# Moving the gates, the weight loads and some decoding around the first experts of a fused attention, MoE and MLP kernel

## The chip, the cores and the metric

The kernel runs on one core of a Trainium2 chip. The metric is the device time of one execution in microseconds (us), as the median of several runs. TensorE has two clock levels, 1.2 and 2.4 GHz; the profile shows the granted clock as a share of the higher one.

## The reference

```python
kv   = einsum('bhsd,bhse->bhde', k, v)            # 4 batches, 8 heads, 576 rows, head size 64
out  = einsum('bhsd,bhde->bhse', q, kv)
attn = out / sqrt(mean(out*out, -1) + 1e-6) * g_norm
x    = attn as [2304, 512]

logits = normed(x) @ normed(expert_emb).T / tau   # 8 experts
e      = argmax(logits, 1); gate = softmax(logits)[e]
x[i]   = gate[i] * (relu(x[i] @ w1[e]) @ w2[e])   # w1 512x1024, w2 1024x512, for the one expert of a row

h = x @ w_in                                       # 512 x 2048
g = max(h, 0) + log1p(exp(-abs(h)))
y = g @ w_out                                      # 2048 x 512, float32 result
```

## The kernel before

**Head.** Attention runs over 18 tiles of 128 rows (`tiles`); its steps are ordered by a small list planner (`step`, `list_schedule`), which takes for each step its engine, an estimated duration, what it depends on and a `tail`, a length of work that is known to follow it. Each finished tile `xa` is stored to `xd` in DRAM. `st_xo` multiplies a tile by g_norm and `st_n` (ScalarE) sums its squares into `ssx`, which only the gates need. Six of these tiles come last, behind the routing. The routing (`top1`, `slots`, `tokens`, `count`, `ranks`, `indices`) sorts the experts by their counts, so that rank 0 is the largest; `CAPS` are the row capacities by rank, 368 down to 280. `rk_idx` holds the row numbers of each rank and `rk_e` the expert of each rank. `offsets` works out where each rank's rows stand in the sorted order `x2`; `gates` works out the gate of each row from `ssx` and the logits.

**Experts.** For each rank r: `gather` fetches the rows from `xd` by an indirect DMA of GpSimd, in three parts of up to 128 rows; `transposes` brings them to the column layout and splits them into a high part `xh` (ScalarE) and a low part `xl` (VectorE). For rank 0 this is `first_transposes`, in pieces. A product of two split operands takes three matmuls (`three`). Eight column blocks m of w1 give `hh` (ScalarE, relu) and `hl` (VectorE); then, in eight steps f, w2 is applied into four output tiles `accs`. Column blocks and output tiles share a ring of five PSUM tiles, so the four tiles of `accs` are those that held column blocks 3 to 6. The weights of an expert come as eight tiles of 512 KB, four of w1 and four of w2 (`load_w`, on SyncE's queue; the expert is read from `rk_e`). `split_w` makes `wh` by a cast on ScalarE and `wl` by a subtraction on GpSimd or VectorE. Before the change, rank 0 has tiles 0 and 2 on GpSimd and the six others on VectorE; the other ranks have all on GpSimd.

Work that is not of the expert itself is called from hooks: `hook1(r, m)` after each column block and `hook2(r, f)` after each f step. They split the weights of rank r+1, load those of rank r+2 (some calls later, through `later` and `now`), gather rank r+2, transpose rank r+1, and run pieces of `pre_decode`. That decodes the 64-bit MLP weights in 32 halves of seven steps, one on ScalarE and six on VectorE, for which it uses a temporary tile in PSUM.

**Gates before.** `gates` is called in three lots around `first_transposes`, ahead of the first expert; `gate_table` sorts the gates by rank in three steps. Rank 0's outputs are multiplied by `gate_row` on VectorE; every other rank has its gathered rows scaled on ScalarE (`scale`), rank 1 at m = 5 to 7 of rank 0, and its outputs copied into `x2` by ScalarE. `row_ids` and `store_ids` write the row numbers to DRAM for the final scatter.

**MLP.** Five blocks of 512 columns of `x2` (`split_x`) go through `mlp_step`, two of which run inside the last expert. The outputs are scattered by an indirect DMA with `idx2`, which is made from the stored row numbers and from `own` and `keep` (the case that a capacity is exceeded).

The queues are those of the engines: each takes its instructions in the order written. The order around the change, ahead of the first expert:

```python
    for c in range(3):
        gather(0, c)
    for i in range(2):
        load_w(0, i)
    nc.sync.dma_start(out=seen, in_=xgs[0][0:1, 2, 0:1])   # holds SyncE until the third part has landed
    for i in range(2, 8):
        load_w(0, i)
```

Of the kernel before, what the change touches and what calls it, by code (L numbers as in the profile page):

```python
# [17 lines left out]
ALU = mybir.AluOpType  # L18
# [7 lines left out]
def attention_moe_mlp(tc, q, k, v, g_norm, emb, tau, w1, w2, w_in, w_out, out, caps=CAPS):  # L26
# [108 lines left out]
    gate_row, ga_row, rf_row = (early[:, 76 * NT + 384 * i:76 * NT + 384 * i + 384] for i in range(3))  # L135
# [50 lines left out]
    with ExitStack() as hs:  # L186
# [223 lines left out]

        def st_xo(t, eng):
            if eng == "G":
                nc.gpsimd.tensor_tensor(out=xo_t[t % NXO], in0=xa_t[t], in1=g_rep.rearrange("p h d -> p (h d)"), op=ALU.mult)
            else:
                nc.vector.tensor_tensor(
                    out=xo_t[t % NXO].rearrange("p (h d) -> p h d", d=D),
# [123 lines left out]
        def indices():  # L540

            pt = tp.tile([128, E, 3, E], F32, name="pt")
            nc.vector.tensor_tensor(
                out=pt,
                in0=tab.rearrange("p e c -> p c e").unsqueeze(1).to_broadcast([128, E, 3, E]),
                in1=perm.unsqueeze(2).to_broadcast([128, E, 3, E]),
                op=ALU.mult,
            )
            yield
            with nc.allow_low_precision("small integers"):  # L550
                nc.vector.tensor_reduce(out=rk_idx, in_=pt, axis=AX.X, op=ALU.add)
            yield
# [51 lines left out]
        def route(g):  # L604
# [18 lines left out]
            if last_:  # L623
# [6 lines left out]
                step(("idx", 0), "D", 269, lambda g_=gen_: next(g_), ("tab", g), ("rank", 4))  # L630
                step(("idx", 1), "D", 269, lambda g_=gen_: next(g_), ("idx", 0), tail=5000)
# [29 lines left out]
        for u in range(NXD, NT):  # L661
            step(("xo", u), "D", 700, lambda u=u: st_xo(u, "D"), ("idx", 1), ("xa", u), ("nn", u - NXO))
            step(("nn", u), "A", 613, lambda u=u: st_n(u), ("xo", u))
# [99 lines left out]
        drain(offsets())  # L763
    head.close()

# [333 lines left out]

    def first_transposes():  # L1100
# [5 lines left out]
        def transposes_of(c):  # L1106
            n = min(128, C - 128 * c)
            for kk in range(KD):
                nc.tensor.transpose(parts[-1][kk][:, 128 * c:128 * c + n], xgs[0][:n, c, kk * 128:kk * 128 + 128], ident[:n, :n])
# [37 lines left out]
    def gate_rows():  # L1147

        ga = ga_row.rearrange("p (c n) -> p c n", n=128)
        nc.vector.tensor_copy(ga, rk_gate[:, 0, :].unsqueeze(2).to_broadcast([128, 3, 128]))  # L1150
        yield
        p = tp_tile()
        for c in range(3):
            n = min(128, caps[0] - 128 * c)
            nc.tensor.transpose(p[:, c * 128:c * 128 + n], ga[:n, c, :], ident[:n, :n])
        nc.scalar.copy(gate_row[:, :caps[0]], p[:, :caps[0]])
        yield

    gr = gate_rows()
# [20 lines left out]

    def hook1(r, m):
        now()
        if r == 0:
            if m in (2, 3):
                next(gq)
            if m in (4, 7):
                next(gr)
            if m in (1, 5):
                next(ri)
            if SC <= m < SC + 3:  # L1190
                scale(1, m - SC)
# [7 lines left out]
        if m % 2 == 1:  # L1199
            first_half(r, m // 2 - (r == 0))  # L1200

    def hook2(r, f):
        now()
        if r + f == 0:
            first_half(r, 3)
# [7 lines left out]
        if 2 <= f < 6:  # L1213
# [3 lines left out]
        if f == 4:  # L1217
            store_ids(r)
        if r == E - 1:
            if f < KD:  # L1220
                split_x(0, f)
# [8 lines left out]
    def expert(r):  # L1230
# [4 lines left out]
        for m in range(NM1):  # L1235
# [8 lines left out]
            if r in (1, 7):  # L1244
# [10 lines left out]
        if r:  # L1255
            off = nc.scalar.value_load(rk_off[0:1, r:r + 1], min_val=0, max_val=XCOL - C)
        if r == E - 1:
# [173 lines left out]
```

## Time and profile before

| | |
|---|---|
| time, median of 3 runs | 740.52 us (740.25 to 741.89) |
| the profiled execution's own time | 742.71 us |
| its span, first to last instruction | 740.9 us |
| mean granted clock of TensorE | 0.982 |
| busy: TensorE, VectorE, ScalarE, GpSimd | 705.3, 514.8, 407.7, 265.1 us |

The rows below come from the profiled execution; times in them count from the start of its span. PE is TensorE, PEld its weight loads, DVE VectorE, ACT ScalarE, POOL GpSimd, and SPq the DMA queue of SyncE. An instruction's row gives its start, its duration, its engine, its line in the kernel, its operation, the tiles that it writes and reads, and their shapes. A bracket says how long the engine was idle before it and what ended that. L872 is the subtraction that makes `wl`, L870 the cast that makes `wh`.

### The profile page before, as it was taken

The numbers are of one execution on the slowest core, as the hardware profiler recorded it, in microseconds if no ns is written. First come the engines' busy times: TensorE is split into PE (matmuls) and PEld (weight loads), VectorE is DVE, ScalarE is ACT, GpSimd is POOL, SyncE is SP. The second block draws the span as 40 slices with busy tenths as digits, with TensorE's granted clock in tenths as the row PEclk, the third lists the DMA queues.
The fourth block names the chain that finished last, engine by engine and source line by source line (L and its number), as shares of the span: only waits on it lengthen the run. The fifth ranks groups of instructions, "written<-read, shape, count | busy, mean of one in ns | idle before, by whom it ended". The sixth has DMA issues, their size and how long they took to land. (4 is left out here: it accounts for less than half of the span.)

```text
span 740.9 us, 11430 instructions
## 1 busy us (share of the span) xinstructions
PE 705.3 (95%) x4180; PEld 619.2 (84%) x4180; DVE 514.8 (69%) x944; ACT 407.7 (55%) x753; POOL 265.1 (36%) x201
## 2 busy tenths in 40 slices
PE   7987489999999999998999999999999999999995
PEld 4977289989999999997888888888888888888894
DVE  3579894988688788897787665656656656566563
ACT  2768466547656567565564654436444454445553
POOL 6234457766786877673463020000200020000201
PEclk9999789999999999999999999999999999999999
DMA  8994599898797988830220010000100000000100
GB/s 240 274 264 168 180 311 315 245 324 267 266 301 258 330 275 290 304 106 32 82 86 31 0 58 1 0 1 1 57 1 0 1 36 22 1 1 0 58 1 32
DMA packets 66912, 96.66 MB, mean 130 GB/s; under 512 B 12948, under 2 KB 41644, under 8 KB 66850
## 3 DMA queue, kind: packets, MB, share of 16 engines
q1 hardware_dynamic: 63330, 86.02, 37.3%
q0 software_dynamic: 3344, 9.80, 3.6%
q8 instruction: 35, 0.57, 0.3%
q14 instruction: 27, 0.22, 0.1%
q10 hardware_dynamic: 176, 0.05, 0.0%
HBM read 78.01 MB, written 17.84 MB: 129 GB/s over the span
## 5 line engine op out<-in xcount | busy, mean ns | idle before, releaser
L872 POOL TENSOR_TENSOR wl<-st,wh 128x1024 fp32r<-128x1024 f32 x66 | 159.6, 2420 | 73.4 <-ACT wh L870 72.8
L977 POOL DMA_INDIRECT out_dram<-orow,idx x18 | 18.5, 1028 | 317.2 <-ACT orow L976 314.1
L940 DVE TENSOR_SCALAR u<-e 128x512 f32<-128x512 f32 (+1 forms) x78 | 31.1, 399 | 123.6 <-ACT e L939 123.5
L938 ACT ACTIVATE e<-tp_t 128x512 f32<-128x512 f32 (+1 forms) x76 | 42.5, 559 | 127.9 <-PE tp_t L866 127.8
L870 ACT CAST wh<-st 128x1024 fp32r<-128x1024 f32 x72 | 75.3, 1047 | 45.5 <-POOL wl L872 21.0
L864 PE MATMUL acc_t<-hh,wh 128*128 128x368 f32 (+7 forms) x256 | 81.2, 317 | 1.7 <-DVE hl L1246 1.6
L864 PE MATMUL acc_t<-xh,wh 128*128 128x368 f32 (+7 forms) x256 | 79.4, 310 | 2.6 <-DVE xl L1117 2.3
L865 PE MATMUL acc_t<-xl,wh 128*128 128x368 f32 (+7 forms) x256 | 78.9, 308 | 0.0
L866 PE MATMUL acc_t<-xh,wl 128*128 128x368 f32 (+7 forms) x256 | 78.8, 308 | 0.0
L865 PE MATMUL acc_t<-hl,wh 128*128 128x368 f32 (+7 forms) x256 | 78.0, 305 | 0.0
L866 PE MATMUL acc_t<-hh,wl 128*128 128x368 f32 (+7 forms) x256 | 78.0, 305 | 0.0
L946 ACT ACTIVATE u<-u 128x512 f32<-128x512 f32 (+1 forms) x78 | 46.1, 591 | 44.0 <-DVE e L942 43.3
L959 DVE TENSOR_TENSOR gl<-u,gh 128x512 fp32r<-128x512 f32 (+1 forms) x78 | 58.0, 743 | 3.0 <-ACT gh L958 3.0
L865 PE MATMUL tp_t<-xs,wh 128*128 128x512 f32 (+1 forms) x160 | 59.0, 369 | 0.6 <-DVE xs L882 0.6
L866 PE MATMUL tp_t<-xs,wl 128*128 128x512 f32 (+1 forms) x160 | 58.9, 368 | 0.0
L864 PE MATMUL tp_t<-xs,wh 128*128 128x512 f32 (+1 forms) x160 | 58.8, 368 | 0.0
L990 PE MATMUL acc_t<-wh,gl 128*128 128x512 f32 x144 | 56.2, 391 | 1.3 <-DVE gl L959 1.3
L988 PE MATMUL acc_t<-wh_b,gh 128*128 128x512 f32 x144 | 56.2, 390 | 0.6 <-ACT gh L958 0.6
L866 PE MATMUL tp_t<-xs,wl_b 128*128 128x512 f32 (+1 forms) x152 | 56.6, 372 | 0.0
L865 PE MATMUL tp_t<-xs,wh_b 128*128 128x512 f32 (+1 forms) x152 | 56.6, 372 | 0.0
L864 PE MATMUL tp_t<-xs,wh_b 128*128 128x512 f32 (+1 forms) x152 | 56.6, 372 | 0.0
L988 PE MATMUL acc_t<-wh,gh 128*128 128x512 f32 x144 | 56.1, 390 | 0.0
(260 smaller groups left out, 1808.4 us busy)
## 6 DMA issues: line engine op xcount, KB each, us to landing
st<-in_moe_w_dram SPq DMA_DIRECT2D x64, 512.0 KB
raw<-in_moe_w_in_dram SPq DMA_DIRECT2D x16, 512.0 KB
raw<-in_moe_w_out_dram SPq DMA_DIRECT2D x16, 512.0 KB
wd<-pre_p SPq DMA_DIRECT2D x32, 256.0 KB
q<-in_q_dram SPq DMA_DIRECT2D x4, 1024.0 KB
xd<-xa SPq DMA_DIRECT2D x16, 256.0 KB
st<-wd SPq DMA_DIRECT2D x8, 512.0 KB
raw<-wd SPq DMA_DIRECT2D x8, 512.0 KB
```

Source lines behind the costliest of these rows:

```text
L864: nc.tensor.matmul(ps_, wh, xh, start=start, stop=False)
L865: nc.tensor.matmul(ps_, wh, xl, start=False, stop=False)
L866: nc.tensor.matmul(ps_, wl, xh, start=False, stop=stop)
L870: nc.scalar.copy(h, raw)
L872: eng.tensor_tensor(out=l, in0=raw, in1=h.bitcast(F32), op=ALU.subtract)
L938: nc.scalar.activation(out=e, in_=h, func=AF.Abs)
L940: nc.vector.tensor_scalar(out=u, in0=e, scalar1=1.0, scalar2=None, op0=ALU.add)
L946: nc.scalar.activation(out=u, in_=u, func=AF.Ln)
L959: nc.vector.tensor_tensor(out=gl, in0=u, in1=gh.bitcast(F32), op=ALU.subtract)
L977: nc.gpsimd.indirect_dma_start(out=rows_out[i], out_offset=bass.IndirectOffsetOnAxis(ap=idx2[:, i:i + 1], axis=0), in_=o, in_offset=None)
L988: nc.tensor.matmul(mt[b][t_], gh[:, cs_], wh[:, f % 2, :], start=f == 0, stop=False)
L990: nc.tensor.matmul(mt[b][t_], gl[:, cs_], wh[:, f % 2, :], start=False, stop=f == NF - 1)
```

## The change

- Rank 0's loads: only tile 0 is issued ahead of `seen`, and `seen` reads the first part of the gather.
- `indices` is done for rank 0 first and then for the others; its four steps have new estimates and tails.
- Matmuls without a use for the result are added: four in `ranks` (`fill`), and four, four and three between the parts of `first_transposes` (`warm`).
- The squares of the last three row tiles are summed later, from tiles of their own (`late_xo`, `late_n`).
- `offsets` runs its first step ahead of the experts and the others at f = 1 of rank 0.
- `gates` runs in fives at m = 1 to 4 of rank 0; `gate_table` at m = 6 and f = 3.
- Rank 0's weight tiles 0, 2, 3 and 5 are subtracted on GpSimd, 1, 4, 6 and 7 on VectorE. Rank 1's gathers come at m = 2 of rank 0.
- Rank 1 is not scaled on its rows; its outputs are multiplied by a `gate_row1` on VectorE, which is made at m = 4 and 6 of rank 1.
- Eight decode steps of rank 1's column blocks go to its f steps (four) and to the last f step of ranks 2 to 5.
- `store_ids` is called at f = 6 instead of 4; `own` and `keep` are made in rank 2, `idx2` after the seventh MLP step; `split_x` of the first block begins one hook earlier.

```diff
+    gate_row, ga_row, rf_row, gate_row1 = (early[...] for i in range(4))
+    late_xo = [early[:, 76 * NT + 1152 + DM * i:76 * NT + 1152 + DM * i + DM] for i in range(3)]
...
             nc.tensor.matmul(cnt, ones, acc, start=True, stop=True)
+            fill(o_t[0][:, 0:2, :].rearrange("p j n -> p (j n)"), 4)
...
+            for a, z in ((0, 1), (1, E)):
+                nc.vector.tensor_tensor(out=pt[:, a:z], ..., op=ALU.mult)
+                yield
+                nc.vector.tensor_reduce(out=rk_idx[:, a:z], in_=pt[:, a:z], axis=AX.X, op=ALU.add)
+                yield
...
-                step(("idx", 0), "D", 269, lambda g_=gen_: next(g_), ("tab", g), ("rank", 4))
-                step(("idx", 1), "D", 269, lambda g_=gen_: next(g_), ("idx", 0), tail=5000)
+                step(("idx", 0), "D", 140, lambda g_=gen_: next(g_), ("tab", g), ("rank", 4), tail=6000)
+                step(("idx", 1), "D", 140, lambda g_=gen_: next(g_), ("idx", 0), tail=6000)
+                step(("idx", 2), "D", 370, lambda g_=gen_: next(g_), ("idx", 1), tail=3000)
+                step(("idx", 3), "D", 350, lambda g_=gen_: next(g_), ("idx", 2), tail=3000)
...
-        drain(offsets())
+        ofs = offsets()
+        next(ofs)
...
+    def late_n(i):
+        nc.scalar.activation(out=late_xo[i], in_=late_xo[i], func=AF.Square, accum_out=ssx[:, NT - 3 + i:NT - 2 + i])
+    def warm(w, n):
+        for _ in range(n):
+            nc.tensor.matmul(w[:, 0:256], ones, ones.unsqueeze(1).to_broadcast([128, 2, 128]), start=True, stop=True)
...
+        parts.append([acc_tile(), acc_tile(), tp_tile(), tp_tile()])
         for c in range(2):
             transposes_of(c)
+            warm(parts[1][2 + c], 4)
         for kk in range(3):
             high(0, kk)
-        parts.append([acc_tile(), acc_tile(), tp_tile(), tp_tile()])
         transposes_of(2)
+        warm(parts[1][0], 3)
...
+    def first_hook1(m):
+        if m == 0:
+            late_n(2)
+            split_rank(0, 2, nc.gpsimd)
+            load_w(1, 2)
+        if m == 1:
+            split_rank(0, 3, nc.gpsimd)
+            load_w(1, 3)
+        if 1 <= m < 6:
+            for _ in range(5):
+                next(gts, None)
+        if m in (3, 5):
+            next(ri)
+        if m in (2, 4):
+            split_rank(0, 3 + m // 2, nc.vector if m == 2 else nc.gpsimd)
+            later(LAG, load_w, 1, 3 + m // 2)
+        if m == 2:
+            for c in range(3):
+                gather(1, c)
+        if m == 6:
+            next(gq)
+        if m in (5, 7):
+            first_half(0, m // 2 - 2)
+    def first_hook2(f):
+        if f in (0, 2):
+            split_rank(0, 6 + f // 2, nc.vector)
+            later(LAG, load_w, 1, 6 + f // 2)
+        if f in (0, 1):
+            first_half(0, 2 + f)
+        if f == 1:
+            drain(ofs)
+        if f == 3:
+            next(gq)
+            next(gq)
+        if f in (4, 6):
+            next(gr[0])
...
     def hook1(r, m):
         now()
         if r == 0:
-            if m in (2, 3):
-                next(gq)
-            if m in (4, 7):
-                next(gr)
-            if m in (1, 5):
-                next(ri)
-            if SC <= m < SC + 3:
-                scale(1, m - SC)
-            if m % 2 == 0:
-                split_rank(0, 4 + m // 2, nc.vector)
-                later(LAG, load_w, 1, 4 + m // 2)
+            first_hook1(m)
         else:
...
+            if r == 1 and m in (4, 6):
+                next(gr[1])
+            if m % 2 == 1:
+                first_half(r, m // 2)
+            if r == E - 1 and m == NM1 - 1:
+                split_x(0, 0)
...
     def hook2(r, f):
+        if r == 1 and f % 2 == 1 or 2 <= r < 6 and f == NM1 - 1:
+            next(pre, None)
-        if f == 4:
+        if f == 6:
             store_ids(r)
+        if r == 2 and f == 6:
+            nc.vector.tensor_scalar(out=own, in0=row_id, scalar1=over, ...)
+            nc.vector.tensor_scalar(out=keep, in0=over, ...)
...
-            if r in (1, 7):
+            if r == E - 1:
                 next(pre, None)
...
-            elif r:
+            elif r > 1:
                 nc.scalar.copy(x2[:, m, ds(off, C)], accs[m][:, :C])
             else:
-                nc.vector.tensor_tensor(out=x2[:, m, 0:C], in0=accs[m][:, :C], in1=gate_row[:, :C], op=ALU.mult)
+                at = ds(off_v, C) if r else slice(0, C)
+                nc.vector.tensor_tensor(out=x2[:, m, at], in0=accs[m][:, :C], in1=gate_of[r][:, :C], op=ALU.mult)
...
-    for i in range(2):
-        load_w(0, i)
-    nc.sync.dma_start(out=seen, in_=xgs[0][0:1, 2, 0:1])
-    for i in range(2, 8):
+    load_w(0, 0)
+    nc.sync.dma_start(out=seen, in_=xgs[0][0:1, 0, 0:1])
+    for i in range(1, 8):
         load_w(0, i)
     gts = gates()
-    for _ in range(5):
-        next(gts)
     fill(tp_tile(), 18)
     split_rank(0, 0, nc.gpsimd)
     load_w(1, 0)
     next(pre)
-    for _ in range(5):
-        next(gts)
     first_transposes()
+    late_n(0)
+    late_n(1)
     split_rank(0, 1, nc.vector)
     load_w(1, 1)
-    for _ in gts:
-        pass
-    split_rank(0, 2, nc.gpsimd)
-    load_w(1, 2)
-    for c in range(3):
-        gather(1, c)
-    next(gq)
-    split_rank(0, 3, nc.vector)
-    load_w(1, 3)
```

## Rows read from the trace of the kernel before

**Rows 1.** TensorE's waits, 95 to 480 us: total, times, longest.
```profile
PE acc_t L864 <- DVE xl L1117: 2.3, 1, 2.3
PE acc_t L864 <- DVE hl L1246: 1.6, 1, 1.6
PE acc_t L990 <- DVE gl L959: 1.3, 1, 1.3
PE tp_t L865 <- DVE xs L882: 0.6, 1, 0.6
```
**Rows 2.** Windows: length, busy time (instructions) by engine; clock, DMA share, GB/s.
```profile
90.00:95.00 5.00, 1.79 (x12) 1.23 (x12) 4.11 (x12) 4.17 (x13) 2.35 (x1) 0.87 0.43 140
95.00:100.00 5.00, 4.27 (x13) 4.02 (x14) 4.96 (x12) 3.51 (x6) 1.85 (x1) 0.50 1.04 321
100.00:105.00 5.00, 5.00 (x44) 4.83 (x43) 4.79 (x11) 2.68 (x6) 4.23 (x4) 0.95 1.04 382
105.00:110.00 5.00, 5.00 (x31) 5.00 (x31) 4.97 (x9) 3.17 (x5) 0.96 (x1) 1.00 1.06 357
```
**Rows 3.** Timeline of SyncE's queue, 84 to 94 us.
```profile
85.34 1.07 SPq L1064 DMA_DIRECT2D st<-in_moe_w_dram  x2
92.82 0.30 SPq L1272 DMA_DIRECT2D seen<-xgt  x1
93.34 1.02 SPq L1064 DMA_DIRECT2D st<-in_moe_w_dram  x2
```
**Rows 4.** Timeline of TensorE and ScalarE, 85 to 103 us.
```profile
86.02 0.63 ACT L423 ACTIVATE junk<-xo 128x512 f32<-128x512 f32 x1 [8.31 <-DVE xo L415]
...
89.79 0.63 ACT L423 ACTIVATE junk<-xo 128x512 f32<-128x512 f32 x1
...
91.39 0.63 PE L1109 MATMUL acc_t<-ident,xgt 128*128 128x128 f32 x4 [1.86 <-DMA xgt<-xd,rk_idx]
...
94.62 0.63 ACT L1113 ACTIVATE xh<-tp_t,gcol 128x112 fp32r<-128x112 f32 x2
...
95.73 0.65 PE L864 MATMUL acc_t<-xh,wh 128*128 128x368 f32 x1 [2.27 <-DVE xl L1117]
...
97.02 1.05 ACT L870 CAST wh<-st 128x1024 fp32r<-128x1024 f32 x1 [0.61 <-DMA st<-in_moe_w_dram]
...
102.56 0.47 ACT L1241 ACTIVATE hh<-acc_t 128x368 fp32r<-128x368 f32 x1
```
**Rows 5.** Timeline of VectorE, 88 to 100 us.
```profile
88.89 0.22 DVE L714 TENSOR_TENSOR below<-rank,io 128x64 f32<-128x64 f32 x1
...
92.50 2.25 DVE L740 TENSOR_TENSOR zt<-lg_all,mx_all 128x144 f32<-128x144 f32 x1
...
95.10 2.14 DVE L1117 SCALAR_TENSOR_TENSOR xl<-acc_t,gcol,xh 128x256 fp32r<-128x256 f32 x6
...
97.64 1.21 DVE L872 TENSOR_TENSOR wl<-st,wh 128x1024 fp32r<-128x1024 f32 x1
...
99.10 2.03 DVE L749 TENSOR_SCALAR gate_all<-gate_all 128x18 f32<-128x18 f32 x1
```
**Rows 6.** Timeline of GpSimd, 92 to 102 us.
```profile
92.24 2.35 POOL L872 TENSOR_TENSOR wl<-st,wh 128x1024 fp32r<-128x1024 f32 x1 [2.87 <-ACT wh L870]
...
98.15 2.95 POOL L872 TENSOR_TENSOR wl<-st,wh 128x1024 fp32r<-128x1024 f32 x1 [3.56 <-ACT wh L870]
```
**Rows 7.** Timeline of GpSimd and VectorE in the MLP, 382 us.
```profile
382.12 3.46 POOL L911 TENSOR_TENSOR wl_b<-raw,wh_b 128x512 fp32r<-128x512 f32 x2 [1.99 <-ACT wh_b L909]
382.64 1.79 DVE L959 TENSOR_TENSOR gl<-u,gh 128x512 fp32r<-128x512 f32 x1
```
**Rows 8.** Timeline of VectorE at the end of the first and of the last expert.
```profile
133.24 1.88 DVE L1265 TENSOR_TENSOR x<-acc_t,early 128x368 f32<-128x368 f32 x4
...
345.31 1.46 DVE L1308 TENSOR_SCALAR own<-row_id,over 128x18 f32<-128x18 f32 x1
...
347.02 0.69 DVE L959 TENSOR_TENSOR gl<-eu,gh 128x512 fp32r<-128x512 f32 x1
```

More of the change, by code (lines that the diff above doesn't have):

```diff
@@ L134, in attention_moe_mlp @@
     chk_all = early[:, 64 * NT:76 * NT].bitcast(BF16).rearrange("p (t n) -> p t n", n=3 * E)
-    gate_row, ga_row, rf_row = (early[:, 76 * NT + 384 * i:76 * NT + 384 * i + 384] for i in range(3))
+    gate_row, ga_row, rf_row, gate_row1 = (early[:, 76 * NT + 384 * i:76 * NT + 384 * i + 384] for i in range(4))
+    late_xo = [early[:, 76 * NT + 1152 + DM * i:76 * NT + 1152 + DM * i + DM] for i in range(3)]
     over = const.tile([128, 1], F32, name="over")
@@ L409, in st_xa, with xo_of @@
                 nc.sync.dma_start(out=xd[lo * S:lo * S + 512, :].rearrange("(p c) n -> p c n", c=4)[:, c, :], in_=xa)
+        def xo_of(t):
+            return late_xo[t - NT + 3] if t >= NT - 3 else xo_t[t % NXO]
         def st_xo(t, eng):
@@ L415, in st_xo @@
                 nc.vector.tensor_tensor(
-                    out=xo_t[t % NXO].rearrange("p (h d) -> p h d", d=D),
+                    out=xo_of(t).rearrange("p (h d) -> p h d", d=D),
                     in0=xa_t[t].rearrange("p (h d) -> p h d", d=D),
@@ L542, in indices @@
             pt = tp.tile([128, E, 3, E], F32, name="pt")
[L543 to L552, printed above, removed]
+            for a, z in ((0, 1), (1, E)):
+                nc.vector.tensor_tensor(
+                    out=pt[:, a:z],
+                    in0=tab.rearrange("p e c -> p c e").unsqueeze(1).to_broadcast([128, z - a, 3, E]),
+                    in1=perm[:, a:z].unsqueeze(2).to_broadcast([128, z - a, 3, E]),
+                    op=ALU.mult,
+                )
+                yield
+                with nc.allow_low_precision("small integers"):
+                    nc.vector.tensor_reduce(out=rk_idx[:, a:z], in_=pt[:, a:z], axis=AX.X, op=ALU.add)
+                yield
         w_ = qp_t[0].rearrange("p j n -> p (j n)")
@@ L1108, in transposes_of @@
             for kk in range(KD):
-                nc.tensor.transpose(parts[-1][kk][:, 128 * c:128 * c + n], xgs[0][:n, c, kk * 128:kk * 128 + 128], ident[:n, :n])
+                nc.tensor.transpose(parts[c // 2][kk][:, 128 * c:128 * c + n], xgs[0][:n, c, kk * 128:kk * 128 + 128], ident[:n, :n])
         def high(u, kk):
@@ L1153, in gate_rows @@
         for c in range(3):
-            n = min(128, caps[0] - 128 * c)
+            n = min(128, caps[r] - 128 * c)
             nc.tensor.transpose(p[:, c * 128:c * 128 + n], ga[:n, c, :], ident[:n, :n])
-        nc.scalar.copy(gate_row[:, :caps[0]], p[:, :caps[0]])
+        nc.scalar.copy(gate_of[r][:, :caps[r]], p[:, :caps[r]])
         yield
-    gr = gate_rows()
+    gate_of = [gate_row, gate_row1]
+    gr = [gate_rows(r) for r in range(2)]
     ri = row_ids()
@@ L1216, in hook2 @@
             next(pre, None)
-        if f == 4:
+        if r == 1 and f % 2 == 1 or 2 <= r < 6 and f == NM1 - 1:
+            next(pre, None)
+        if f == 6:
             store_ids(r)
+        if r == 2 and f == 6:
+            nc.vector.tensor_scalar(out=own, in0=row_id, scalar1=over, scalar2=None, op0=ALU.mult)
+            nc.vector.tensor_scalar(out=keep, in0=over, scalar1=-1.0, scalar2=1.0, op0=ALU.mult, op1=ALU.add)
         if r == E - 1:
-            if f < KD:
-                split_x(0, f)
+            if f < KD - 1:
+                split_x(0, f + 1)
             elif f in (M0, M0 + 2):
@@ L1306, in attention_moe_mlp @@
     nc.sync.dma_start(out=idx2, in_=dtab[0:NTOK].rearrange("(t p) o -> p (t o)", p=128))
-    nc.vector.tensor_scalar(out=own, in0=row_id, scalar1=over, scalar2=None, op0=ALU.mult)
-    nc.vector.tensor_scalar(out=keep, in0=over, scalar1=-1.0, scalar2=1.0, op0=ALU.mult, op1=ALU.add)
-    nc.vector.scalar_tensor_tensor(out=idx2, in0=idx2, scalar=keep, in1=own, op0=ALU.mult, op1=ALU.add)
     ms = ExitStack()
@@ L1317, in attention_moe_mlp @@
         mlp_step(s)
+        if s == 6:
+            nc.vector.scalar_tensor_tensor(out=idx2, in0=idx2, scalar=keep, in1=own, op0=ALU.mult, op1=ALU.add)
     mlp_end()
```

21 lines of the change are left out of this document (10 added, 11 removed).

## The prediction

> **What bounds the kernel now.** I read the waits of TensorE first, from the start of the experts on. TensorE is busy almost without a break from 95.7 us to the end, and only four waits over 0.5 us are left there: 2.3 us before the first expert matmul, 1.6 us for hl, 1.3 us for gl and 0.6 us for xs [rows 1]. So the end moves by what changes before the first expert runs at full speed, by these waits, and by any new wait that the moved work puts in front of TensorE.
>
> Then the windows around the head's end. In 90 to 95 us TensorE is busy for only 1.79 of 5 us; its granted clock falls, and in all of 95 to 100 us it is 0.50, the 1.2 GHz level. From 100 to 105 us it is 0.95, from 105 us on 1.00, 2.4 GHz [rows 2]. The 13 matmuls of 95 to 100 us are thus paid at 4.27/13 = 0.33 us each and not at the 5.00/31 = 0.161 us of 105 to 110.
>
> The queues show why TensorE starts late. SyncE issues two weight tiles at 85.34, waits for the third gather (seen, 92.82) and issues the other tiles from 93.34 on [rows 3]. The first transpose waits for the first gather until 91.39; the first expert matmul starts at 95.73, held by xl, and the relu of column block m = 1 starts at 102.56 [rows 4]. xl itself was not late for want of data. VectorE has offsets from 88.89 on, then gate steps; one of these (L740, 128x144) sits for 2.25 us, and only at 95.10 does the first xl come [rows 5]. GpSimd's wl of tile 0 runs from 92.24 to 94.59 [rows 6]: L740 ends just behind it. The gate step L749, on 128x18, lasts 2.03 us in the same way behind the wl that starts at 98.15.
>
> **Part by part.**
> *Start of the first expert.* One 512 KB tile fewer lies in front of the gathers: at 357 to 382 GB/s [rows 2] 1.4 us. The index of rank 0 comes out of 24 and 3 columns a partition instead of 192 and 24, some 0.3 us earlier; descriptor writing bounds that, so I take 1.4 us in all for the three landings (bounds 0.4, the index alone, and 1.8). The eight high parts ended at 95.25 (94.62 plus 0.63) [rows 4], 3.9 us behind the first landing. Behind a landing at 90.0 they end at about 94.0, the warm matmuls (11 of 256 columns, in gaps where TensorE waits anyway) adding 0.2 at most. Since offsets (but one step) and gates no longer stand ahead of the low parts, the last low ends 0.3 to 0.5 us later, at 94.5, and block m = 0 ends at 95.3. If the clock is up, m = 1 ends at 97.4 (12 x 0.161 = 1.94 more, and 0.1 for the start of a block) against 102.4: **minus 5.0 us**. Of this 13 x (0.33 - 0.161) = 2.2 is the clock. The four fills behind the count run where TensorE waits for VectorE; priced at zero; if the token matmuls had to wait for them, some 0.2 us. Bounds: minus 2.8, the clock as before, and minus 5.6.
>
> The later issue of tile 1 (behind the first gather, so at about 90.6) does not bind: a tile issued at 93.34 was cast at 97.02, 3.7 us later [rows 3, 4]; tile 1 is then there at 94.3, and ScalarE is free for it only at 95.5, behind two of the moved squares ((89.79 - 86.02)/5 = 0.75 each [rows 4]). VectorE's split, 1.21 us [rows 5], ends at about 97.9, 0.3 us behind the first use of m = 2; that is in the estimate of the f loop's start below.
>
> *The gate pieces and the splits inside the first expert.* This is the unknown. VectorE must read column blocks m = 3 to 6 (hl) before the four output tiles of the f loop can be opened, since these take the same PSUM tiles. In my chain TensorE opens the f loop at 97.4 + 6 x 1.94 + 0.8 (split, row ids, block starts) = 109.8, and wants hl of m = 5 by 110.8. VectorE: its first gate step follows hl of m = 1 at 99.5; ScalarE has by then done three squares and the casts of tiles 1 and 2 (1.05 each [rows 4]), so GpSimd's wl of tile 2 holds 98.8 to 101.1 and that of tile 3 101.2 to 103.5 (2.35 each [rows 6]). Each catches one gate step. Then come the gathers, in which nothing is caught, and VectorE has left 15 small steps at 0.21 (0.22 alone [rows 5]), four hl at 0.47 (as the multiplies of that shape, 1.88 for four [rows 8]) and one split of 1.2: free, hl of m = 5 ends at 109.7, in time.
>
> But tile 5's wl is GpSimd's. Its cast stands behind the gates' exponential, which is due at 105.8 (103.5, seven small steps, two of them 144 wide, and one hl), a small copy and a relu (0.47 [rows 4]); with the cast's 1.05 some 2.2 us in all, so the wl starts at 108.0. VectorE has by then done the split, hl of m = 3 and three more steps, and still has five. The trace shows how two such queues mix: where GpSimd issues two subtractions back to back (382.12) VectorE's operations of two SBUF tensors pass one for each: the one at 382.64 takes 1.79 us, while its like at 347.02 takes 0.69 [rows 7, 8]. So one step passes at 110.4 and the next at 112.75, behind the wl of the second expert's tile 0. The cast of its tile 1 stands behind the relu of m = 7 and an eleventh 512 KB transfer; I have it ready near 111.8, too close to 112.75 to call. I take two steps caught and the rest free: 112.75 + 3 x 0.21 + 0.47 = 113.85 against 110.8, **plus 3.0 us**. Bounds: 0 (VectorE 1.7 us ahead of my chain) and 9 (each of the five steps behind one wl of 2.35, and more of this further on, where offsets stand ahead of tile 7's split).
>
> The Trainium skill states the same as a rule and speaks against this change: in "SBUF — State Buffer", section "Who interferes with whom", whoever of VectorE (in a two-port mode, or with two SBUF inputs) and GpSimd issues first has the shared port pair for the whole instruction, and the other blocks fully. The trace agrees (2.03 us for 128x18 [rows 5]); by this rule alone, with GpSimd never idle, the sum would be that of the slower rival below.
>
> *Second expert.* In the first half of expert 1 eight of 24 decode steps go, which removes the lag of VectorE behind the 1.6 us [rows 1]: **minus 1.6** (bounds 0 and minus 1.7). Four of them come in its f loop and four later, where VectorE has idle time; zero. The outputs of expert 1 are now four VectorE multiplies and no ScalarE copies; TensorE's first block of expert 2 has a free PSUM tile and covers them, otherwise 1.9 us, the four of them. Three scalings leave ScalarE, where nothing waited for them: zero. The second gate row adds three transposes to TensorE's path: 3 x 0.16 (0.63 for four [rows 4]): **plus 0.5**.
>
> *Into the MLP.* The own, keep and idx2 steps stood ahead of gl: own took 1.46 us at 345.31, gl started at 347.02 [rows 8]. But gl reads two SBUF tensors, and own was held by a wl that ended at about 346.7; gl would be held too, so **minus 0.3** of the 1.3 (bounds 0 and minus 1.3). split_x comes one f step earlier in the order, yet its casts waited for no f step; zero, with the 0.6 us of rows 1 as bound to both sides.
>
> *Other moved steps.* store_ids two f steps later holds back SyncE's later weight loads only if offsets are late; they have a whole expert of lead: zero, otherwise 1 us. The second expert's gathers go behind tile 3's wl; their rows are wanted only by transposes in the f loop: zero. The late squares are wanted only by the gates.
>
> Sum: -5.0 + 3.0 - 1.6 + 0.5 - 0.3 = **-3.4 us**, against the profiled execution's 742.71 (span 740.9 and 1.8 around it): 739.3. The runs shown have a median of 740.52, 2.2 below; carried there, **737.1 us**.
>
> **Rivals.** *VectorE is not caught* (its steps come 1.7 us earlier, or tile 5's cast later): the 3.0 goes, 734.1. For: 1.7 us is little in so long a chain. Against: the sequence behind the exponential is the same on both engines.
> *Slower: the alternation goes on.* Place: behind the wl of expert 1's tile 0. Condition: the cast of its tile 1 is done before 112.75. Then VectorE passes one step per 2.35 us, hl of m = 5 comes at 118 to 119, and tgb, offsets and the split of tile 7 go the same way: 8 to 10 us in place of 3.0, so 742 to 744. For: VectorE was busy 4.97 of 5 us in 105 to 110 already [rows 2]. Against: with TensorE waiting GpSimd runs out of tiles, since their buffers are still in use.
> *The warm matmuls do not hold the clock.* The first expert starts at 0.50 as before and gives 2.2 back: 739.3. For: in 90 to 95 us some work was there too and the clock fell. Against: with the 11 matmuls TensorE is nearly without gaps from the first landing on.
>
> **How the numbers follow.** Forecast case 0.40, not caught 0.22, alternation 0.28, clock 0.10. A run tells 0.2% (1.5 us) from no change, so 739.0 and 742.0 are the borders. Faster: 0.38 + 0.22 + 0.02 (alternation cut short) + 0.03 = 0.65. Same: 0.02 + 0.06 + 0.06 = 0.14. Slower: 0.20 + 0.01 = 0.21. Range: from 733.4 (not caught, with the earlier landing) to 743.4, inside the alternation case; the forecast case alone spans 735.5 to 738.5.
>
> **What would show it.** Granted clock 1.00 in 95 to 100 us and the relu of m = 1 near 97.5: the start. TensorE's wait for hl at the first f step: 3 us the forecast, none or 8 the rivals; VectorE's 128x18 steps of about 2.3 us in 98 to 120 us, counted, tell which. No wait for hl in expert 1. The prediction is wrong if the gathers land no earlier (then 1.4 us go), or if TensorE waits for gate_row's transposes or for tile 6 or 7's split in the f loop.

## The result and the profile after

The changed kernel takes 748.41 us (median of 5 runs, 746.55 to 749.23) against 740.52 us (median of 5 runs, 740.25 to 741.89): ratio 1.0091, interval 1.007 to 1.0113. The prediction, 737.1 us and at most 743.4, had the wrong sign: 3.4 us less were forecast, 7.9 more came. The profiled execution is the fastest of the five, 746.55 us with a span of 744.8, so between the two profiles only 3.9 of the 7.9 us are to be seen: the profiled execution of before lies 2.2 above its median, that of after 1.9 below. What that hides comes with the experiments and at the end of the part on the prediction.

First TensorE's waits of the changed kernel from 88 to 480 us: in all, times, longest.

```profile
PE acc_t L877 <- DVE hl L1305: 5.9, 2, 4.3
PE acc_t L877 <- DVE x L1325: 1.4, 1, 1.4
PE acc_t L1003 <- DVE gl L972: 0.9, 1, 0.9
PE tp_t L1109 <- DVE xl L1111: 0.5, 1, 0.5
```

The 2.3 us ahead of the first expert and the 1.6 us for hl in the second [rows 1] are gone. In their place stand 5.9 us for hl and 1.4 us for x. The windows (columns as in rows 2) give the place:

```profile
95.00:100.00 5.00, 5.00 (x31) 5.00 (x31) 3.74 (x4) 3.85 (x7) 2.39 (x2) 1.00 1.04 367
105.00:110.00 5.00, 4.95 (x30) 4.57 (x28) 4.90 (x6) 3.45 (x7) 4.82 (x3) 1.00 1.09 366
110.00:115.00 5.00, 0.77 (x3) 0.46 (x3) 4.97 (x4) 3.73 (x4) 5.00 (x3) 0.93 1.00 335
115.00:120.00 5.00, 3.37 (x11) 3.37 (x12) 4.93 (x8) 0.00 (x0) 4.02 (x3) 0.50 0.51 166
120.00:125.00 5.00, 5.00 (x30) 4.97 (x29) 4.93 (x11) 2.55 (x3) 2.06 (x1) 0.89 0.26 89
```

In 95 to 100 us TensorE now has 31 matmuls at clock 1.00 where there were 13 at 0.50 [rows 2]. But in 110 to 115 us it has 3, with VectorE and GpSimd both "busy" throughout, and in the next 5 us the clock is 0.50. The timelines of GpSimd, ScalarE, VectorE and TensorE there:

```profile
106.33 9.34 POOL L885 TENSOR_TENSOR wl<-st,wh 128x1024 fp32r<-128x1024 f32 x4
...
109.85 3.87 ACT L883 CAST wh<-st 128x1024 fp32r<-128x1024 f32 x4
...
106.72 4.39 DVE L764 CAST gp<-gate_all 128x18 bf16<-128x18 f32 x1
111.02 0.53 DVE L1305 SCALAR_TENSOR_TENSOR hl<-acc_t,hh 128x368 fp32r<-128x368 f32 x1
111.48 1.94 DVE L768 TENSOR_TENSOR left<-gate_all,gp 128x18 f32<-128x18 f32 x1
113.45 2.26 DVE L764 CAST gp<-left 128x18 bf16<-128x18 f32 x1
115.75 0.18 DVE L768 TENSOR_TENSOR left<-left,gp 128x18 f32<-128x18 f32 x1
115.96 0.18 DVE L764 CAST gp<-left 128x18 bf16<-128x18 f32 x1
116.05 0.53 DVE L1305 SCALAR_TENSOR_TENSOR hl<-acc_t,hh 128x368 fp32r<-128x368 f32 x1
...
116.63 0.68 PE L877 MATMUL acc_t<-hh,wh 128*128 128x368 f32 x1 [4.26 <-DVE hl L1305]
117.72 0.51 PE L877 MATMUL acc_t<-hh,wh 128*128 128x368 f32 x1
```

Read it by the durations. GpSimd runs four wl in one unbroken row (tile 5 of the first expert, then tiles 0, 1, 2 of the second), about 2.33 us each. A cast of 128x18, 0.18 us at 115.96, takes 4.39 us at 106.72, to the end of the second wl; the next two steps take 1.94 and 2.26, one wl each. Such a step is called held below. These 8.6 us stand in front of hl, and when TensorE starts again at 116.63 it spaces its matmuls by 0.31 us; up to 121.1, 14 of them cost 14 x (0.31 - 0.17) = 2.0 us more.

Start times of the first matmul of each expert put the change into stretches. Given are the lengths from the first transpose to the first matmul, of the first, second and third expert, and of what follows:

```
              transposes   expert 1   expert 2   expert 3   rest of the span
before        4.34         37.04      33.94      30.51      543.7
after         3.42         44.41      32.35      32.23      543.4
```

The first expert starts 3.3 us earlier (92.40 against 95.73) and then takes 7.4 us more, its f loop alone 27.5 us against 17.5; the second takes 1.6 us less, the third 1.7 us more: -3.3 + 7.4 - 1.6 + 1.7 - 0.3 = +3.9. Of the 10.0 us more in the f loop 5.9 are the waits for hl and 2.0 the clock; 1.5 are the matmuls of the gate table and the gate row, which the change moved there from the column blocks.

### The profile page after: what moved, and what is told of

Its sections match the earlier page's. It is cut to its first block, busy times and chain, and to the rows that moved or that the text cites. A ratio compares the mean times of both kernels' runs of the same rounds, so it can differ in the third digit from the quotient of the medians.

```text
span 744.8 us, 11467 instructions
## 1 busy us (share of the span) xinstructions
PE 708.0 (95%) x4198; PEld 619.5 (83%) x4198; DVE 529.1 (71%) x949; ACT 404.1 (54%) x747; POOL 269.0 (36%) x203
## 5 line engine op out<-in xcount | busy, mean ns | idle before, releaser
L885 POOL TENSOR_TENSOR wl<-st,wh 128x1024 fp32r<-128x1024 f32 x68 | 163.4, 2408 | 74.8 <-ACT wh L883 73.9
L879 PE MATMUL acc_t<-hh,wl 128*128 128x368 f32 (+7 forms) x256 | 78.8, 308 | 0.0
```

What stands on the lines that cost most here:

```text
L879: nc.tensor.matmul(ps_, wl, xh, start=False, stop=stop)
L885: eng.tensor_tensor(out=l, in0=raw, in1=h.bitcast(F32), op=ALU.subtract)
```

## The experiments

The theory: VectorE's small steps that read and write SBUF are held while GpSimd runs its row of wl, and hl stands behind them. Rivals: VectorE has simply too much to do; the transfers are late; the clock costs the time. Diffs are against the changed kernel unless another one is named. Lengths of the experts are worked out as above.

**1. Gate steps in PSUM (a1_psum).** The same steps in the same order, one operand of nearly each in a PSUM tile.

```diff
+            gp_ps = mp.tile([128, 512], F32, name="gp_ps", tag="acc5")
-            gt = gate_all
+            gt = gp_ps[:, 2 * NT:3 * NT]
```

> The changed kernel with the small gate tensors in one PSUM tile, so that every VectorE gate step but the first and the first zt step has one operand in PSUM (two small ScalarE copies more, the order on VectorE unchanged). Theory (the gate steps of two SBUF tensors take turns with GpSimd's back-to-back wl): the steps that took 4.39, 1.94 and 2.26 us fall to about 0.2 to 0.3 us each, hl of m = 4 to 6 come in time, the two f-loop waits of 1.66 and 4.26 us and the half clock behind them go: 8 to 10 us less, 737 to 740 us. Rival (VectorE has simply too much to do, or hl waits for something else): the waits for hl stay within 1 us and the time stays at 746 to 749 us.

Measured 750.58 us (ratio to before 1.0128, 1.0106 to 1.015): the time is the rival's, the mechanism is not. VectorE's and GpSimd's timelines:

```profile
98.35 4.77 POOL L899 TENSOR_TENSOR wl<-st,wh 128x1024 fp32r<-128x1024 f32 x2 [5.62 <-ACT wh L897]
99.14 1.65 DVE L162 TENSOR_SCALAR n_x<-ssx 128x18 f32<-128x18 f32 x1
101.53 0.18 DVE L171 TENSOR_TENSOR gp_ps<-gp_ps,n_r 128x18 f32<-128x18 f32 x1 [0.74 <-ACT gp_ps L169]
...
106.34 0.18 DVE L778 CAST gp<-gp_ps 128x18 bf16<-128x18 f32 x1 [0.24 <-issue]
107.28 0.17 DVE L782 TENSOR_TENSOR gp_ps<-gp_ps,gp 128x18 f32<-128x18 f32 x1
...
107.81 10.61 POOL L899 TENSOR_TENSOR wl<-st,wh 128x1024 fp32r<-128x1024 f32 x4 [0.87 <-ACT wh L897]
...
107.92 0.18 DVE L778 CAST gp<-gp_ps 128x18 bf16<-128x18 f32 x1
109.91 6.24 DVE L797 TENSOR_TENSOR tgb<-early,gp 128x432 bf16<-128x432 bf16 x3
119.94 5.08 DVE L748 TENSOR_TENSOR nr<-nr,capt 128x8 f32<-128x8 f32 x1
125.46 3.05 DVE L753 SCALAR_TENSOR_TENSOR rk_off<-nr,over,offf 128x8 int32<-128x8 f32 x1
```

Of the gate steps only the first, n_x, which has no operand in PSUM, is still held (1.65 us); those with one take 0.18 us beside wl (101.53, 107.92), and no wait for hl is left. But the next VectorE steps on SBUF tensors are held: tgb 6.24 us for three, then two offsets of 128x8 for 5.08 and 3.05. In the first expert TensorE now waits once, and longer, for xl of the second expert, which stands behind them:

```profile
PE tp_t L1123 <- DVE xl L1125: 10.5, 1, 10.5
```

**2. GpSimd's second-expert splits later (a2_pool).** `first_half(0, 0..3)` at f = 0 to 3 in place of m = 5, 7 and f = 0, 1.

> The changed kernel with GpSimd's splits of the second expert's tiles 0 to 3 put into the f loop (f = 0 to 3) in place of m = 5, m = 7, f = 0 and f = 1: the same VectorE steps in the same order, but only one wl (tile 5's) near them. Theory: of the gate steps one or two are held, by one wl of 2.35 us; the wait for hl falls from 5.9 to at most 1.5 us, the time by 5 to 8 us to 739 to 743 us, unless the splits are late for the second expert (a wait for wl near 130 us would show that). Rival (amount of VectorE work): no change, 746 to 749 us.

753.52 us (1.016), 10 us over what was expected. The same answer: the wait for hl falls to 0.2 us, and with the row of wl moved on, an offset is caught, from 0.4 us ahead of the row to the end of all three:

```profile
119.06 7.42 DVE L736 TENSOR_TENSOR nr<-nr,capt 128x8 f32<-128x8 f32 x1
...
119.46 6.98 POOL L885 TENSOR_TENSOR wl<-st,wh 128x1024 fp32r<-128x1024 f32 x3
```

The wait for xl is 12.5 us. "Too much work on VectorE" falls with these two: its steps are the same, and the waits move with what stands beside GpSimd's row.

**3. No warm matmuls (a3_nowarm).** The 11 calls of `warm` left out.

> The changed kernel without the 11 warm matmuls between the first transposes. If they hold the clock, the granted clock in 95 to 100 us falls from 1.00 towards 0.50 and the first expert's relu of m = 1 comes about 2.2 us later, at 99.6 us; since VectorE and GpSimd set the f loop's start, the end then moves by less than that, 0 to 1 us. If they hold nothing, the clock stays at 1.00 and the time at 746 to 749 us.

746.80 us (1.0094, 1.0057 to 1.013), no difference from the changed kernel. The granted clock is 1.00 in each window from 85 to 110 us without them: in this run they hold nothing. What goes with the clock is the gap ahead of the first expert, closed by the earlier xl: experiment 7's e3, the kernel before without warm matmuls and with that gap at 0.7 us in place of 2.3, shows 1.00 in 95 to 100 us too. The same trace shows what the profiled execution of after does not:

```profile
103.51 9.35 POOL L885 TENSOR_TENSOR wl<-st,wh 128x1024 fp32r<-128x1024 f32 x4
...
103.62 0.27 DVE L760 RECIPROCAL gate_all<-gate_all 128x18 f32<-128x18 f32 x1
103.92 9.00 DVE L764 CAST gp<-gate_all 128x18 bf16<-128x18 f32 x1
```

The first gate cast is held over all four wl, and the wait for hl is 8.9 us, not 5.9. In a4_fill it is held 8.98 us, in e2_order 8.99. The fastest execution of the changed kernel let it in behind two. That the slower executions of that kernel look like these three is likely, and not shown, as they have no profile.

**4. The wait filled (a4_fill).** 5 and 16 matmuls of `fill` in front of the second and third output tile.

> The changed kernel with 5 matmuls of 512 columns in front of the second and 16 in front of the third output tile of the first expert's f loop, where TensorE waits 1.66 and 4.26 us for hl. They take the place of idle time. Theory: the waits as such stay, but the matmuls behind them run at 0.16 and not at 0.31 us; some 13 of them at 0.15 us: 2 us less, 744.5 to 746.5 us. Rival (the clock is no part of the loss): no change, or up to 1 us more where the filling outlasts the wait.

751.38 us, where 744.5 to 746.5 were expected. Inconclusive: the 16 matmuls waited 2.8 us for rk_rows, which reads the PSUM tile that they write, and ran 5.56 us themselves, at first at the low clock. The share of the clock is thus only read from the spacing above, 2.0 us.

**5. Offsets ahead again, then tgb from PSUM, then the decoding (c1_ofs, c2_tgb, c3_dec).** Each on top of the one before, the first on a1_psum. The first hunk is c1's, the second c2's (`gpp` is in PSUM, and tgb reads it), the third c3's:

```diff
-        ofs = offsets()
-        next(ofs)
+        drain(offsets())
...
+                nc.scalar.copy(gpp[u], gparts[u])
...
-        if r == 1 and f % 2 == 1 or 2 <= r < 6 and f == NM1 - 1:
+        if 2 <= r < 6 and f in (3, NM1 - 1):
             next(pre, None)
```

> The kernel with the gate steps in PSUM, and the offsets (eight small VectorE steps on SBUF) back where they stood before the change, ahead of the first low parts. The run with the gate steps in PSUM showed the holds passed on: tgb 6.24 us for three, then offsets of 128x8 held 5.08 and 3.05 us, and a wait of TensorE of 10.5 us for xl of the second expert. Theory (whatever VectorE step of two SBUF tensors stands beside the back-to-back wl is held): the offsets' 8 us go, the wait for xl falls to 1.5 to 4 us (tgb is still held), the time by 6 to 9 us to 741.5 to 744.5 us. Rival (xl is late for another reason, the splits or the transfers): the wait for xl stays over 8 us and the time within 1.5 us of 750.6.

> As the run before this one in the list, and the three tgb multiplies read the gate pieces from PSUM (three small ScalarE copies more). Theory: tgb takes 1.6 us as before the change and not 6.24 us, the wait for xl falls below 1 us, nothing is left of the loss in the first expert and the gain of the start (5 us) and of the second expert (1.6, less the 1.4 us wait for its outputs) comes through: 736 to 739 us. Rival: as that run, within 1 us.

> As the run before this one in the list, and the four decode steps of the second expert's f loop put off to the third to sixth expert (one each at f = 3). Theory: the second expert's four output multiplies then follow its last matmul at once, the third expert's wait for x (1.4 us in the changed kernel) falls below 0.5 us, and the time by 1.0 to 1.4 us. Rival (the multiplies themselves, 1.75 us for four, are the wait): the wait stays over 1 us and the time the same.

742.26 (1.0024, 0.9995 to 1.0053), 745.66 and 745.25 us. c1's time is as expected, and its interval holds no difference from the kernel before; c2 and c3 missed what was expected of their times. The first expert falls from 48.6 to 40.8 us in c1 and 38.7 in c2 (39.3 in c3), so the first two steps take holds away; but in c2 and c3 the second takes 37.9 us. There ScalarE's cast of the second expert's tile 7 waits 8.13 us (c2) for its transfer with the first relu behind it. With c3 the third expert falls from 32.28 to 30.58 us: the 1.4 us for x are the decode steps in front of the multiplies, as the theory had it, though the whole time hides it.

The early offsets also showed a reader of theirs that the prediction missed. SyncE's queue loads the overflow flag (over_i), which is made of them, ahead of `seen`. Its waits in c1, and in the kernel before from 84 to 96 us, where the profile names n_x, the step right behind the flag:

```profile
SPq L1381 <- DVE over_i L754: 6.9, 1, 6.9
```

```profile
SPq L1324 <- DVE n_x L161: 4.3, 1, 4.3
SPq L1272 <- DMA xgt<-xd,rk_idx: 1.7, 1, 1.7
```

**6. The kernel before with the earlier gathers alone (d1_head):** one weight tile ahead, `seen` on the first part, the index in two pieces.

> The kernel before with two parts of the change alone: one weight tile ahead of the gathers and SyncE's wait on the first gather, and the index table in two pieces. The prediction's theory of the start: the three landings come 1.4 us earlier (bounds 0.4 and 1.8), but the first expert matmul is held by VectorE's offsets and gate steps (one of them behind GpSimd's wl), so at most 1.4 us of the 5.0 us come: 739.5 to 741.5 us. Rival (the landings are all that holds the start): 4 to 5 us less, 736 to 737 us.

741.23 us, ratio 1.0001 (0.9984 to 1.0019): as expected, nothing. SyncE waits 5.2 us for the offsets and TensorE 3.6 us for xl behind the gate step. Alone, the earlier gathers do not make the start: VectorE's offsets and gates still stand in front. What they are worth in the change is worked out below.

**7. Order alone (e2_order, and e3_before on the kernel before).** e2: `drain(ofs)` behind `first_transposes` and the decode steps as in c3. e3: the second five gate steps and the offsets there, the decode steps later.

> The changed kernel with two steps moved alone: the offsets behind the first low parts, and the four decode steps out of the second expert's f loop; the gate steps stay in SBUF. Theory (the gate steps themselves are held beside wl): the wait of 5.9 us for hl at the start of the f loop stays (4 to 9 us); of the time only the 1.4 us for x and some tenths go: 745.5 to 748 us. Rival (the offsets were the cause): 738 to 742 us.

> The kernel before with three moves of VectorE's order and nothing else of the change: the second five gate steps and the offsets behind the first low parts in place of ahead of them, and the eight additional decode steps of the second expert put into the third to sixth expert. Theory: the first expert matmul no longer waits for VectorE's gate step of 2.25 us, so it starts 2 to 3 us earlier, and SyncE, which waited 4.3 us for the offsets ahead of the third gather, issues the weight tiles 1 to 2 us earlier; the wait of 1.6 us for hl in the second expert goes: minus 3 to minus 5 us, unless the moved steps are held in front of hl: 736 to 738.5 us. Rival (the landings hold the start, and the moved steps come back as waits for hl): within 1 us of the kernel before.

e2: 746.10 us, as expected, with a wait for hl of 9.2 us: the gate steps by themselves. e3: 742.41 us (1.0004, 0.9984 to 1.0025), the rival's time. The first matmul stands 2.6 us behind the first transpose, not 4.3, and the second expert takes 32.0 us, not 33.9; but the first takes 41.0 us: the moved steps make tgb late (a wait of 3.4 us).

**8. Everything moved (e1_all), and the loads' order (e4_loads).** e1 is a1 with tgb from PSUM, the offsets behind the first low parts, the gate table at f = 2, row ids at m = 2 and 4, the gate row at f = 4 and 7, and the decode steps as in c3. e4 adds:

```diff
-            later(LAG, load_w, 1, 6 + f // 2)
+            load_w(1, 6 + f // 2)
-            later(LAG, load_w, r + 2, i)
+            later(LAG if r else LAG + 3, load_w, r + 2, i)
```

> The changed kernel with the gate steps and the gate pieces in PSUM, the offsets right behind the first low parts (VectorE has 1.4 us idle there in the changed kernel, GpSimd has no wl, and SyncE's load of the overflow flag, which stood in front of the weight tiles in the run with early offsets, comes behind them), the gate table's matmuls one f step and the row ids one column block earlier, the gate row one f step later, and the four decode steps out of the second expert's f loop. Theory: no wait of TensorE over 1 us is left between the first and the third expert; the first expert takes about 39 us from its first matmul as before the change and not 46.5, and the time is 734 to 738 us, under both kernels. Rival (what the waits gave is taken by the next one, as in the two runs before): 740 us or more.

> As the run with everything moved (742.44 us), and two changes of the order of SyncE's loads in the first expert: the second expert's tiles 6 and 7 are issued as soon as their buffers are read, and the third expert's first four tiles three hooks later, so that tile 7 no longer stands behind them. In that run the first expert took 36.5 us, as in the kernel before, but the second 36.9 and not 32.0, because ScalarE's cast of its tile 7 waited 4.3 us for the transfer and the relu of the first column block stood behind that cast. Theory (the gain of the start is there and is lost to that transfer): the cast waits under 1 us, the second expert takes 32 to 33 us, and the time is 737.5 to 739.5 us, under both kernels by 0.3 to 0.6%. Rival (the transfers as a whole, not their order, are late): the second expert still takes over 35 us, or the third takes 2 us more than 30.5; no change, 741 to 743 us.

742.44 us (1.0, 0.9981 to 1.002) and 744.85, both the rival's times; e1 is back at the kernel before. Its first expert takes 36.5 us, below before's 37.0. How VectorE's tgb, with the pieces in PSUM, runs inside GpSimd's row, and what is late next:

```profile
110.10 11.45 POOL L902 TENSOR_TENSOR wl<-st,wh 128x1024 fp32r<-128x1024 f32 x4 [3.09 <-PE acc_t L896]
...
112.19 1.62 DVE L800 TENSOR_TENSOR tgb<-early,gp_ps 128x432 bf16<-128x432 bf16 x3
...
134.74 1.05 ACT L900 CAST wh<-st 128x1024 fp32r<-128x1024 f32 x1 [4.32 <-DMA st<-in_moe_w_dram]
```

The second expert takes 36.9 us. In e4 that cast waits no more, and the second expert takes 39.6 us: its scaling waits 5.5 us for gathered rows. The order of the loads was not the cause. The reading that is left, that GpSimd's queue, from which loads and gathers get their turn, was behind, is tested next.

**9. The two splits back on VectorE (f3_undo in the changed kernel, f1_splits in e1, f2_loads with tile 6 and 7 loaded at once).** The change had given tiles 3 and 5 of the first expert to GpSimd.

```diff
-            split_rank(0, 3, nc.gpsimd)
+            split_rank(0, 3, nc.vector)
-            split_rank(0, 3 + m // 2, nc.vector if m == 2 else nc.gpsimd)
+            split_rank(0, 3 + m // 2, nc.vector)
```

> The changed kernel with one part undone: the splits of the first expert's tiles 3 and 5 are VectorE's again, as before the change (1.2 us each there, 2.35 us each on GpSimd). Theory (the splits that the change moved to GpSimd make the unbroken row of wl, and the row holds the gate steps): GpSimd has 4.7 us less to do before the second expert's tiles, VectorE 2.4 us more; the held steps become fewer, the wait for hl falls from 5.9 to 1 to 4 us and the time by 2 to 6 us to 742.5 to 746.5 us. Rival (the second expert's own wl follow at once and hold the same steps): the wait stays at 5 us or more, the time within 1.5 us of 748.4.

> The same two splits back on VectorE in the kernel with everything moved (gate steps and pieces in PSUM, offsets behind the first low parts, decode steps put off; 742.44 us). Theory: with GpSimd 4.7 us ahead, the second expert's loads and the third's gathers come so much earlier; the second expert takes 32 to 34 us in place of 36.9, the first stays at 36 to 38 us, and the time is 737 to 740 us, under both kernels. Rival (VectorE's additional 2.4 us come back as waits for hl, or the transfers are late all the same): 741 us or more.

> As f1_splits, and the second expert's tiles 6 and 7 are loaded as soon as their buffers are read (the third expert's first tiles keep their place, unlike in e4_loads). Theory: it takes a last wait of ScalarE's cast of tile 7 away, if f1_splits still has one: 0 to 1.5 us under f1_splits, 736.5 to 739.5 us. Rival: SyncE, waiting for VectorE's splits of tiles 6 and 7, holds back the third expert's tiles: 1 to 3 us over f1_splits.

f3: 750.97 us (1.0118), where 742.5 to 746.5 were expected. The wait for hl falls to 1.2 us, as the theory said, and the time does not, since tgb and a split are caught further on (and xl, 9.8 us):

```profile
114.16 5.92 DVE L783 TENSOR_TENSOR tgb<-early,gp 128x432 bf16<-128x432 bf16 x3
120.44 5.73 DVE L885 TENSOR_TENSOR wl<-st,wh 128x1024 fp32r<-128x1024 f32 x1
```

f1 and f2: 740.23 us (0.9984, 0.9962 to 1.0006) and 740.24, both just over the top of what was expected. The second expert takes 33.2 and 32.4 us in place of 36.9, the first 38.0 and 38.1 in place of 36.5. So it was GpSimd being behind that made the second expert late; in the whole time the step from e1 (1.0) to f1 (0.9984) lies within the intervals. Undoing the splits alone (f3) gives nothing back, moving the steps alone (e1) brings the kernel before's time.

**10. The rest (g2_dec, g1_five).** g2: the four decode steps in the third expert's f loop. g1: also tile 5's split at m = 6, behind hl.

> As f1_splits (740.23 us), and the four decode steps that were put off stand in the third expert's f loop (where the outputs are ScalarE's copies) and not one each in the third to sixth expert. Theory (put off so far, they shifted which decode step stands in front of ScalarE's copies of x): the waits for these copies fall from 1.3 us to 0.5 us or less; the time by 0.5 to 1.5 us to 738.7 to 739.7 us. Rival (the copies waited for something else): no change.

> As g2_dec, and VectorE's split of tile 5 stands behind hl of column block 6 and not between hl of 4 and 5. Theory: the f loop's wait of 1.8 us for hl goes (tile 5 is wanted only at its third step), the time falls by another 1 to 1.8 us, to 737.5 to 738.5 us, under both kernels by 0.4%; with it the prediction's terms for the start and the second expert would be seen in the time. Rival (tile 5's weights or the gate table come late in its place): no change against g2_dec.

739.74 us (0.9979, 0.9961 to 0.9997) and 739.18 us (0.997, 0.9955 to 0.9984): the last is 0.3% under the kernel before, clear of noise, and 1.2% under the changed one, a little short of what was expected. g2's waits for ScalarE's copies are down to 0.3 us. Its profiled execution, 741.4 us of span, has 4.0 us for xl again. g1's waits:

```profile
PE tp_t L1126 <- DVE tg L807: 1.7, 1, 1.7
PE acc_t L894 <- DVE hl L1320: 1.6, 2, 1.1
PE acc_t L1143 <- DMA xgt<-xd,rk_idx: 1.0, 1, 1.0
```

## Why the prediction was wrong

*Start, minus 5.0: right, though 0.9 of it is the execution's luck.* The relu of m = 1 comes at 97.39 against 102.56 [rows 4], 5.2 us earlier, at full clock. How much of this is scatter shows at the matmul that counts the rows of the experts, which stands ahead of the first edited step. It and the first transpose, of before, after and d1:

```profile
81.46 0.17 PE L519 MATMUL misc<-acc,ones 128*128 128x8 bf16 x1 [0.37 <-DVE acc L507]
80.56 0.17 PE L523 MATMUL misc<-acc,ones 128*128 128x8 bf16 x1 [0.37 <-DVE acc L511]
...
88.98 0.60 PE L1126 MATMUL acc_t<-ident,xgt 128*128 128x128 f32 x4
...
82.47 0.17 PE L519 MATMUL misc<-acc,ones 128*128 128x8 bf16 x1 [0.37 <-DVE acc L507]
...
91.42 1.04 PE L1112 MATMUL acc_t<-ident,xgt 128*128 128x128 f32 x8
```

Over the sixteen kernels made from the changed one, itself among them, the count's matmul stands between 78.8 and 83.7 us, so the 0.9 us between before and after are within the scatter. From there to the first transpose pass 9.9 us in before [rows 4], 9.8 in e3, 9.0 in d1 and 8.4 in after: the earlier gathers are worth 1.0 to 1.5 us, as the 1.4 of the sum, also in d1. There the gate step in front of xl takes them back: to the first expert matmul pass 14.3 us in before, 14.5 in d1, 12.4 in e3, which moves offsets and gate steps but not the gathers, and 11.8 in after. The wait at `seen` [rows 3] was read as one for the third gather; 4.3 us of it were for the offsets. The rival on the clock had its condition right (the warm matmuls hold nothing) and its price not: the clock is up without them.

*Gate pieces and splits, plus 3.0: the step that failed.* The sum took from rows 7 that VectorE passes one operation for each wl, and set two steps caught, by 2.35 us each. The profile of after gives: 3.9 at the end, less -5.2 for the start, -1.6, +1.7 and -0.3, leaves +9.3. The chain held as far as the row: the first two wl catch one step each (1.64 us at 98.40, 1.82 at 100.58), and five gate steps are left when tile 5's wl begins. But this begins at 106.33 and not at 108.0, three steps are caught and not two, and the first of them, the cast at 106.72, lasts through two wl, in the kernels with the same order through four (8.98 to 9.00 us). The slower rival had the place (GpSimd going on with the second expert's tiles) and its 8 to 10 us, with a chance of 0.28. Its condition, tile 1's cast done before the wl of tile 0 ends, was met: ScalarE's four casts start at 109.85 and follow each other without a gap, and tile 1's is the first of them. The reason given against it, that GpSimd runs out of tiles, did not hold. Its price of one step per 2.35 us fits the second and third caught step (1.94 and 2.26) and not the first. The trace agrees with the rule of the Trainium skill that was set beside this term ("SBUF — State Buffer", section "Who interferes with whom": the blocked one waits out the whole instruction) in single holds such as the 2.26 us at 113.45; the 9.00 us over four instructions go beyond it. The clock's 2.0 us behind the wait stood in no case.

*Second expert, minus 1.6, second gate row, plus 0.5: right within some 0.3 us each.* Together 1.1 us less were forecast, and it takes 1.6 less; e3, which moves the decode steps without the gate row, takes 1.9 less, which leaves 0.3 for the row.

*Outputs of the second expert on VectorE, 0 with a bound of 1.9: wrong, 1.7.* They wait behind decode steps that the change itself put at the end of that f loop; with these moved, the third expert takes 30.6 us as before. A cover was named (TensorE's free PSUM tile), and it was not checked what VectorE's queue holds at that time.

*gl and xs:* 1.3 to 0.9 us and 0.6 to 0.4; right.

*From the span to the median.* The forecast carried before's offset of 2.2 us along; the profiled execution of after lies 1.9 below its median instead. This other half of the loss stands in no profile of the changed kernel. Two things can make it: whether a held step gets in between two wl (a3 waits 8.9 us for hl, not 5.9), and the scatter ahead of the count's matmul. From that matmul to the end of the span pass 659.4 us in before, 664.2 in after and 665.8 in a3, so +4.8 and +6.3 us of the 7.9; how the rest is shared is open.

## What to carry to other kernels

Before small VectorE steps are moved into a stretch, list what GpSimd has queued there without a gap, and price a step that can be held at the whole row (9.00 us over four here), not at one instruction; an operand in PSUM takes a step out of this. Removing one held step passes the hold to the next one in the queue: a1 and a2 gave nothing back. c1 and e1, which took more of them away, are back at the time of the kernel before within their intervals, and only g2 and g1, with GpSimd's two splits back on VectorE and the rest moved, are below it, by 0.2 and 0.3%. And look at what reads a moved value in the other queues: here a flag for a branch at the end stood in front of the weight loads.

## What was not expected of the hardware

VectorE does not always get its turn between two GpSimd operations: one cast of 128x18 (0.18 us alone) was held 4.39 us over two of them in one execution and 9.00 us over four in another, a step of 128x8 for 7.42 us. With one operand in PSUM such steps took 0.17 or 0.18 us beside wl (a1), and three of 128x432 took 1.62 us (e1) in place of 6.24 (a1). GpSimd pays too when VectorE gets in: its row of four took 9.34 us where VectorE was mostly held, 11.45 us in e1, where two wl of VectorE (1.77 and 1.51 us) ran inside it.

Not every step from SBUF to SBUF is held. The reciprocal at 103.62 in a3 takes 0.27 us inside the row that then holds the cast for 9.00, and a reduce in before takes 0.29 us inside the wl of 98.15 to 101.10 [rows 6] that holds the step behind it for 2.03 [rows 5]:

```profile
98.77 0.29 DVE L747 TENSOR_REDUCE gate_all<-zt 128x18 f32<-128x144 f32 x1
```

Held were steps with two SBUF inputs, and casts and TENSOR_SCALAR steps with one.
